# Making an exactness flag ahead of the last stores, and hinting the branch that depends on it

## The chip, the cores and the metric

The kernel runs on one core of a Trainium2 chip. Its metric is the device time of one execution in microseconds (us). That time is longer than the span that a profile shows, which goes from the first to the last instruction of the kernel.

Engines: PE is TensorE, DVE is VectorE, ACT is ScalarE, POOL is GpSimd, SP is SyncE. A small q (SPq) marks an instruction that the engine's sequencer handles alone.

Some words that recur: an *instruction packet* is a packet of a DMA queue that the profile lists as instruction (8 or 16 KB each in these traces); I read it as an engine's next instructions and call those of one packet a *block*. The *hole* behind a branch is the time from the start of the branch to the start of the engine's next instruction. The *issue* of a store is the time that SyncE spends on starting it, and the store has *landed* at the last landing that the profile records for it.

## The reference

```python
xn = layernorm(x)                          # 2048 x 512
s  = multi_query_attention(xn, wq, wk, wv) @ wo   # 32 heads of 16, softmax over 2048 keys
g  = silu((silu(xn @ w_gate) * (xn @ w_up)) @ w_down)
out = x + s * g
```

## The kernel before

The kernel computes the softmax without a row maximum. That is exact as long as the denominators stay in a range, so it checks them at the end: one flag, loaded into a register of every engine, and a branch. If the flag is set, an exact path with row maxima computes everything again. With these inputs it never is, and every engine jumps over the exact path. GpSimd has no instruction in that path, SyncE some 185, the others thousands (counted in e10_forced, the one run that executed it).

```python
    for i, o in enumerate(order):          # the body: instructions in a fixed order
        ...
        r = o.emit()
        chain(o.eng if o.eng != "DMA" else "SP", r)
    ...
    tadd("DVE", ...)                       # dlc = (denominators are in range)
    for k in range(2):
        tadd("PE", e_out_mm(LN + k, obk[k], [NQ - 1]))
    for k in range(2, 4):
        tadd("PE", e_out_mm(LN + k, obk[k], [NQ - 1]))
    tadd("DVE", e_out_mul(LN, obk[0], dsts[0]))
    fin_add(0, nc.gpsimd, "POOL")
    ...                                    # three more multiplies and adds
    fin_add(3, nc.vector, "DVE")
    for k in range(4):
        tadd("SP", e_out_st(LN + k))       # the last four stores
    tadd("DVE", nc.vector.tensor_reduce(out=fmin[:, 2:3], in_=dlc[:], ...))
    tadd("DVE", nc.vector.tensor_reduce(out=fmin[:, 3:4], in_=fmin[:, 0:3], ...))
    tadd("PE", nc.tensor.matmul(out=tq01[0:1, 0:1], lhsT=fmin[:, 3:4], rhs=ones_f[:], ...))
    tadd("DVE", nc.vector.tensor_single_scalar(out=flag_i[:], in_=tq01[0:1, 0:1], scalar=P - 0.5, op=ALU.is_lt))
    ...
    flag = nc.values_load(flag_i[0:1, 0:1], min_val=0, max_val=1)
    with tc.If(flag > 0):
        _exact_max_path(...)
```

`chain` and `tadd` fix the order of issue on one engine.

## Time and profile before

| | before |
|---|---|
| time, median of the first three runs | 783.76 us |
| span of the profiled run | 780.93 us |
| ScalarE, TensorE, VectorE busy | 97%, 96%, 94% |
| last VectorE add ends | 774.24 us |
| flag loaded by all engines from | 775.05 us |
| last store issued, landed | 774.27, 775.98 us |

The prediction shows the lines that carry this. The last 5.9 us have no computing at all: flag loads, the bounds check, a branch with a hole of 2.7 to 4.1 us on every engine but GpSimd (0.17 us), and the closing waits and barrier. One line of the store's source line (shortest, median and longest issue in ns):

```profile
L698 SPq DMA_DIRECT2D out_dram<-xn x4: 332/338/344, 772.2 to 774.3; - x4
```

### The profile page before, as it was taken

What the parts mean: (1) busy time and instruction counts of PE and PEld (TensorE: products, weight loads), DVE (VectorE), ACT (ScalarE), POOL (GpSimd) and SP (SyncE); (2) the same over time, 40 slices, a digit from 0 to 9 for tenths busy, and PEclk for the clock granted to TensorE, in tenths of its full rate; (3) what the DMA queues carried; (4) which work ended last, traced back from release to release, by engine and by line L of the source; (5) the groups of instructions that cost most, each with busy time, mean ns of one, the idle gap of its engine ahead of it and who ended that gap; (6) DMA issues with size and microseconds to landing.
All of it is one profiled execution on the core that took longest, in us unless ns stands there. A gap on an engine that the chain in (4) does not pass through costs nothing.

```text
span 780.9 us, 21436 instructions
## 1 busy us (share of the span) xinstructions
PE 749.8 (96%) x9095; PEld 230.2 (29%) x9095; DVE 735.7 (94%) x920; ACT 757.2 (97%) x866; POOL 53.5 (7%) x59
## 2 busy tenths in 40 slices
PE   8999999999999999999999999999999999999994
PEld 3323223322222333322232322222223333222221
DVE  7689999999999999999999999999999999999994
ACT  6999999999999999999999999999999999999992
POOL 2100000000012000000001110000000300000101
PEclk9999999999999999999999999999999999999997
DMA  9400000000001000000000100000000000000001
GB/s 329 139 8 9 16 2 24 2 8 17 6 27 49 24 2 8 17 2 24 3 10 29 42 23 2 24 1 9 17 2 24 29 22 2 3 23 2 23 2 32
DMA packets 21199, 20.20 MB, mean 26 GB/s; under 512 B 8744, under 2 KB 17192, under 8 KB 21096
## 3 DMA queue, kind: packets, MB, share of 16 engines
q1 hardware_dynamic: 19512, 18.20, 7.7%
q8 instruction: 73, 1.20, 0.6%
q10 hardware_dynamic: 1584, 0.56, 0.3%
q14 instruction: 30, 0.25, 0.1%
HBM read 14.19 MB, written 2.34 MB: 21 GB/s over the span
## 4 chain that ended last, share of the span: by engine, by line
PE 46%; ACT 38%; issue 8%; DVE 6%; SPq 0%; DMA 0%; ACTq 0%; POOL 0%; DVEq 0%; POOLq 0%
ACT Pb L937 33%; PE ring L877 17%; PE m_ps L488 15%; PE o_ps L747 13%; ACT th L657 3%; DVE Bf L991 2%; ACT g_sb L937 1%; DVE Bf L1010 1%; PE ring L433 1%; ACT th L674 1%; DVE x_sb L1010 0%; DVE x_sb L1005 0%; PE ring L488 0%; DVE hT L663 0%; DVE Bf L1005 0%
## 5 line engine op out<-in xcount | busy, mean ns | idle before, releaser
L937 ACT ACTIVATE Pb<-ring 128x1024 bf16<-128x1024 f32 x772 | 726.4, 1141 | 2.5 <-PE ring L877 2.3
L877 PE MATMUL ring<-QB,KT 32*128 32x512 bf16 x2048 | 306.1, 382 | 15.5 <-ACT Pb L937 8.9
L991 DVE TENSOR_SCALAR Bf<-ring 128x1024 uint16<-128x1024 f32 x172 | 209.6, 1218 | 5.4 <-PE ring L877 4.0
L877 PEld LDWEIGHTS <-KT 32*128 32x128 bf16 x2048 | 94.4, 91 | 314.1 <-issue 307.4
L747 PE MATMUL o_ps<-Pb,VA 128*32 128x512 bf16 x1544 | 146.9, 385 | 0.0
L1010 DVE TENSOR_TENSOR Bf<-Bf,Bf 128x2048 f16<-128x2048 f16 x74 | 90.3, 1220 | 0.1
L991 DVE TENSOR_SCALAR x_sb<-ring 128x1024 uint16<-128x1024 f32 x72 | 87.7, 1218 | 2.5 <-PE ring L877 2.1
L747 PE MATMUL o_ps<-xnT,zw 128*32 128x512 bf16 x1092 | 83.1, 381 | 0.0
L488 PE MATMUL m_ps<-xnT,wu_sb 128*32 128x512 bf16 x896 | 72.6, 384 | 0.8 <-DVE ab L659 0.6
L488 PE MATMUL m_ps<-wd_sb,hT 128*32 128x512 bf16 x896 | 71.5, 383 | 0.1
L488 PE MATMUL m_ps<-xnT,wg_sb 128*32 128x512 bf16 x896 | 70.4, 384 | 0.0
L747 PE MATMUL o_ps<-Bf,VD 128*32 128x512 f16 x688 | 67.1, 385 | 0.9 <-DVE Bf L1010 0.5
L732 POOL TENSOR_TENSOR oT<-oa,rb 128x512 bf16<-128x512 f32 x15 | 22.0, 1464 | 615.6 <-DMA rb<-dscr 409.2
L1017 DVE TENSOR_SCALAR Bf<-Bf 128x2048 uint16<-128x2048 uint16 x86 | 62.0, 721 | 0.6
L747 PEld LDWEIGHTS <-VA 128*32 128x32 bf16 x1560 | 38.0, 94 | 53.8 <-issue 51.5
L1005 DVE TENSOR_SCALAR Bf<-Bf 128x2048 uint16<-128x2048 uint16 x74 | 51.2, 700 | 0.0
L659 DVE SCALAR_TENSOR_TENSOR ab<-th,m_ps 128x512 f32<-128x512 f32 x56 | 38.1, 681 | 4.2 <-ACT th L657 3.9
L657 ACT ACTIVATE th<-m_ps 128x512 f32<-128x512 f32 x56 | 40.1, 716 | 0.0
L663 DVE TENSOR_TENSOR hT<-ab,m_ps 128x512 bf16<-128x512 f32 x56 | 38.2, 682 | 2.0 <-PE m_ps L488 1.6
L747 PEld LDWEIGHTS <-VD 128*32 128x32 f16 x976 | 26.5, 94 | 39.4 <-issue 35.8
L747 PEld LDWEIGHTS <-zw 128*32 128x32 bf16 x1092 | 25.8, 95 | 25.5 <-issue 12.9
L1010 DVE TENSOR_TENSOR x_sb<-x_sb 128x2048 f16<-128x2048 f16 x24 | 29.2, 1217 | 0.0
(121 smaller groups left out, 416.3 us busy)
## 6 DMA issues: line engine op xcount, KB each, us to landing
rb<-dscr SPq DMA_DIRECT2D x15, 256.0 KB
out_dram<-xn SPq DMA_DIRECT2D x16, 128.0 KB, 1.9
dn<-oa SPq DMA_DIRECT2D x120, 2.0 KB, 1.7
oa<-oa SPq DMA_DIRECT2D x60, 32.0 KB, 2.0
wg_sb<-in_B_w_gate_dram SPq DMA_DIRECT2D x1, 1792.0 KB, 11.5
wu_sb<-in_B_w_up_dram SPq DMA_DIRECT2D x1, 1792.0 KB
wd_sb<-in_B_w_down_dram SPq DMA_DIRECT2D x1, 1792.0 KB, 20.3
x_sb<-in_A_x_dram SPq DMA_DIRECT2D x3, 512.0 KB
```

The lines of the kernel that those rows point to most:

```text
L488: return [nc.tensor.matmul(out=dst[GRP * j:GRP * j + GRP, :], lhsT=w[:, GRP * j:GRP * j + GRP], rhs=rhs, start=start, stop=stop, tile_posi ...
L657: t_ = OP("ACT", 0.477, [a], lambda: nc.scalar.activation(out=th[i][:], in_=m_ps[:], func=ACT.Tanh, scale=0.5), (0,), name="tanh")
L659: s_ = OP("DVE", 0.6, [t_, ab_rel[i]], lambda: nc.vector.scalar_tensor_tensor(out=ab[i][:], in0=th[i][:], scalar=1.0, in1=m_ps[:], op0=ALU ...
L663: h = OP("DVE", 0.6, [b], lambda: nc.vector.tensor_tensor(out=hT[:, f, :], in0=ab[i][:], in1=m_ps[:], op=ALU.mult), (1,), name="hmul")
L732: return [pk, q], lambda eng: eng.tensor_tensor(out=oT[qs % 2][:, jj, :], in0=o0[:], in1=rbt[:], op=ALU.mult)
L747: r.append(nc.tensor.matmul(out=o_ps[GRP * g:GRP * g + GRP, :], lhsT=lhs, rhs=rhs, start=(n == 0), stop=(n == pv_total[(b, g)] - 1), tile_ ...
L877: return lambda: [nc.tensor.matmul(out=ring[sl][:, u * 512:(u + 1) * 512], lhsT=KT[half][GRP * g:GRP * g + GRP, t * P:(t + 1) * P], rhs=QB ...
L937: lambda: nc.scalar.activation(out=buf, in_=ring[i][:], func=ACT.Exp, scale=escale, bias=ebias),
L991: lambda: nc.vector.tensor_scalar(out=U[:, hs], in0=ring[si][:], scalar1=ubias, scalar2=UINF, op0=ALU.add, op1=ALU.min), (1.5, u), name="p ...
L1005: o1 = OP("DVE", 0.6, [pa, pa0] + wrel, lambda: nc.vector.tensor_scalar(out=Bf[wi], in0=U, scalar1=0x3FF, scalar2=0x3800, op0=ALU.bitwise_and,
L1010: return lambda: eng.tensor_tensor(out=Bf[wi][:, a:z].bitcast(FP16), in0=Bf[wi][:, a:z].bitcast(FP16), in1=U[:, a:z].bitcast(FP16), op=ALU ...
L1017: o2 = OP("DVE", 0.6, o3, lambda: nc.vector.tensor_scalar(out=U, in0=U, scalar1=0x7C00, scalar2=None, op0=ALU.bitwise_and), (2, u, 1), nam ...
```

## The change

Intent: make the flag before the last multiplies, load it before the stores, drop the check that it is 0 or 1, and give each engine a hint ahead of its branch, meant to have the branch's target fetched by then. The whole diff, moved lines shortened:

```diff
     tadd("DVE", nc.vector.tensor_tensor(out=dlc[:], in0=dlc[:], in1=dlf, op=ALU.is_equal))
+    tadd("DVE", nc.vector.tensor_reduce(out=fmin[:, 2:3], in_=dlc[:], ...))
+    tadd("DVE", nc.vector.tensor_reduce(out=fmin[:, 3:4], in_=fmin[:, 0:3], ...))
     ...
     for k in range(2):
         tadd("PE", e_out_mm(LN + k, obk[k], [NQ - 1]))
+    tadd("PE", nc.tensor.matmul(out=tq01[0:1, 0:1], lhsT=fmin[:, 3:4], rhs=ones_f[:], ...))
     for k in range(2, 4):
     ...
     tadd("DVE", e_out_mul(LN, obk[0], dsts[0]))
+    tadd("DVE", nc.vector.tensor_single_scalar(out=flag_i[:], ...))
+    for en, et in (("SP", "SP"), ("POOL", "Pool"), ("PE", "PE"), ("DVE", "DVE"), ("ACT", "Activation")):
+        with tc.issue_after(_last[en].ins):
+            tc.mark_branch_hint_location("exact", "LikelyTaken", [getattr(mybir.EngineType, et)])
+    loads, vals = nc.values_load_multi_w_load_instructions(flag_i[0:1, 0:1])
+    flag = vals[0]
+    tadd("SP", [l for l in loads if l.ins.engine == nc.sync.engine])
     fin_add(0, nc.gpsimd, "POOL")
     ...
     for k in range(4):
         tadd("SP", e_out_st(LN + k))
-    (the two reduces, the matmul and the compare)
-    flag = nc.values_load(flag_i[0:1, 0:1], min_val=0, max_val=1)
-    with tc.If(flag > 0):
+    with tc.If(flag > 0, label="exact"):
```

## The prediction

> **What bounds the kernel now.** I read the page first, for which part of the 780.9 us the change can touch at all. In the body ScalarE is busy 97%, TensorE 96% and VectorE 94%. The main row is 772 exponentials of 1141 ns on ScalarE. None of that is in the diff, and the order of the body is fixed by the kernel's own list, so I take everything up to the last block as unchanged. What is left is the end of the program. I cut it into stretches with the view of busy time by window:

> ```profile
> 766.00:770.00 4.00, 3.46 (x42) 1.26 (x33) 2.26 (x10) 1.02 (x3) 0.00 (x0) 1.00 0.01 4
> 770.00:772.00 2.00, 0.62 (x12) 0.12 (x8) 1.86 (x4) 0.00 (x0) 1.02 (x1) 1.00 0.00 0
> 772.00:775.00 3.00, 0.19 (x2) 0.09 (x2) 2.58 (x7) 0.00 (x0) 1.69 (x2) 0.50 0.40 131
> 775.00:778.00 3.00, 0.00 (x0) 0.00 (x0) 0.02 (x1) 0.00 (x0) 0.00 (x0) 0.50 0.20 58
> 778.00:780.90 2.90, 0.00 (x0) 0.00 (x0) 0.00 (x0) 0.00 (x0) 0.00 (x0) 0.50 0.05 14
> ```

> The columns are the stretch and its length, then busy us and count for TensorE, its weight load, VectorE, ScalarE and GpSimd, then clock, DMA share and GB/s. From 770 to 775 VectorE sets the pace (1.86 of 2, 2.58 of 3). After 775 there are 5.9 us in which no engine computes. So I looked at the instructions that do not count as busy, by the line of the flag load and of the branch:

> ```profile
> L1367 SPq TENSOR_LOAD <-flag_i x1: 482/482/482, 775.1 to 775.1; - x1
> ...
> L1367 SPq FUSED_REGOPS  x1: 192/192/192, 775.6 to 775.6; - x1
> L1367 SPq SEQ_ASSERT  x1: 37/37/37, 775.8 to 775.8; - x1
> ```

> ```profile
> L1368 SPq EVENT_SEMAPHORE  x8: 17/17/17, 779.0 to 779.5; - x8
> L1368 ACTq COMPARE_BRANCH  x1: 50/50/50, 775.6 to 775.6; - x1
> ...
> L1368 PEldq COMPARE_BRANCH  x1: 4038/4038/4038, 775.7 to 775.7; - x1
> L1368 DVEq COMPARE_BRANCH  x1: 72/72/72, 775.7 to 775.7; - x1
> L1368 SPq COMPARE_BRANCH  x1: 50/50/50, 776.2 to 776.2; - x1
> L1368 ACTq EVENT_SEMAPHORE  x1: 17/17/17, 778.4 to 778.4; - x1
> L1368 DVEq EVENT_SEMAPHORE  x1: 21/21/21, 778.8 to 778.8; - x1
> ```

> The three numbers are the shortest, median and longest duration in ns. Every engine loads the flag at 775.05, when VectorE has just made it, in 0.47 to 0.54 us. Then all branch over the exact path. SyncE branches only at 776.24, after the two bounds-check instructions, and the next instruction that it executes starts at 778.99: 2.7 us of nothing. ScalarE has the same hole from 775.64 to 778.40 and VectorE from 775.75 to 778.81; TensorE shows it inside the branch itself, 4.04 us. The trace's instruction-fetch packets (8 KB for SyncE, ScalarE and VectorE, 16 KB for TensorE) run from 776.54 to 778.27, so the hole is the fetch of the branch's target. SyncE's waits say that nothing else holds it:

> ```profile
> SPq L1368 <- SPq L1368: 2.7, 1, 2.7
> SPq L1396 <- PEq L1396: 0.7, 2, 0.5
> ```

> The last store was issued at 774.27 and had landed by 775.98 (1.71 us), before any of this. From SyncE's second semaphore wait after the branch (779.085) to the last instruction (ends 780.93) there are 1.85 us: seven more waits at 0.07, eight double waits at 0.06 each, drains, two rounds of the closing barrier.

> So the chain that ends the program is: last VectorE add, two reduces, a tiny matmul, the compare, the flag load, the bounds check, the branch, the fetch, SyncE's closing waits.

> [...]

> **The change, part by part.** (1) *Flag ahead of the stores.* The two reduces (172 and 156 ns) move to where VectorE idles for 0.63 us before its first multiply (770.14), waiting for TensorE: they cost nothing. The fp32 matmul (two passes, 0.19 us together) goes between the output matmuls at about 770.0; it pushes outputs 2 and 3 by perhaps 0.1 us, and they are finished 0.9 us before VectorE needs them. The compare (146 ns, about 0.2 us from start to start, as the small neighbours at 769.12 and 769.32 are spaced) sits between the first and second multiply of a VectorE that is back to back from 770.14 to 774.24. So the last add ends 0.2 us later, at 774.44. What leaves the path behind the add is 774.24 to 775.05: 0.8 us of reduces, matmul and compare. (2) *Load ahead of the stores.* SyncE's load ends near 771.6, before the first store's data (772.14): free. The 0.48 us leave the end. (3) *No bounds check*: 775.60 to 776.24, about 0.65 us, leaves; but with the load moved it would have stood beside VectorE's work anyway. (4) *Hints.* TensorE and ScalarE now branch near 771.7 and would be through their own fetches by 775.9 and 774.6 even unhinted. VectorE would need till about 776.9. Only SyncE, which branches after the fourth store (774.47 + 0.34 + 0.05 = 774.86), would have its 2.7 us at the end: resume at 777.55.

> New end without a working hint: 777.55 plus the 1.95 us from SyncE's resuming to the end (778.985 to 780.93) = 779.5, a gain of 1.4 us. With the hint SyncE goes on at once and meets the last store instead: issued 774.47, landed 774.47 + 1.71 = 776.18, plus 1.85 us of closing = 778.03, a gain of 2.9 us. That is the central step: the fetch is replaced by the landing of the last store, and half of the hint's 2.7 us is lost to it.

> **Rivals.** *A, VectorE's own flag load gets in the way.* Only SyncE's load is chained. VectorE loads the flag too; if that stands right behind the compare, its sequencer waits for the compare and then 0.54 us, and everything behind moves by some 0.6 us: gain 2.3. For it: it is traced there. Against: in the opening of the trace a VectorE operation that waits for GpSimd is placed behind later-written memsets, so what is ready sooner goes first, and the second multiply is ready. Behind that multiply, the load would mostly hide beside 0.68 us of execution. *B, GpSimd's load stands ahead of its first add*: the add starts at 771.6 in place of 770.98, both GpSimd adds move 0.6 us, and stores 2 and 3 are issued in order behind them: gain about 2.4. *C, the hint does nothing[...]* before SyncE branches: gain 1.4. Only some ten SyncE instructions stand between hint and branch, which speaks against it. *D, the hints hurt*: [...] gain about 0, or a small loss. *E, the prediction that the eye makes*, all 5.9 us gone: impossible, since 1.71 + 1.85 us after the last store remain.

> **Range and chances.** Weights: all as worked out 0.5 (783.76 - 2.9 = 780.9), A or B 0.3 (781.4), C 0.12 (782.4), D 0.08 (783.8). The median is about 781.1. The three runs of before spread by 0.5 us, so the range is 780.4 to 782.4. A 2% change would be 15.7 us; the whole tail is 5.9 us, so neither side of 2% is within reach unless the body's order changed, which the fixed list speaks against.

> **What would show it right or wrong.** Right: the body to 770 us unchanged; SyncE's first semaphore wait comes under 0.2 us after its branch; its wait for the last store ends 1.7 us after that store's issue; last add at 774.4; the span near 778.0. Wrong in step 1: the second multiply starts later than 771.0, with a flag load on VectorE before it. B: GpSimd's load before its first add. C: SyncE still has a hole of 2.7 us behind the branch, and instruction packets lie after it. D: a new hole between hint and branch. Wrong altogether: a body that ended earlier or later by over 1 us.

The gain is 2.9 us, so the time 783.76 - 2.9 = 780.9 us with weight 0.5, and beside it stand the rivals' 781.4 (0.3), 782.4 (0.12) and 783.8 (0.08), for a median near 781.1. That a working hint lets SyncE go on at once was the change's claim; no trace taken before the prediction has a hint in it. The weights, the loss in D and the use made of the ten SyncE instructions in C were my estimates.

## More of the kernel before

All runs but one were fast, with a granted TensorE clock of 0.99 or more; the exception, e10_forced, is no timing.

A *far* branch is one that jumps over the exact path.

## The result, and the profile after

The median is 781.57 us (six runs, 780.87 to 782.02) against 783.49 us (six runs). The ratio is 0.9974, 95% interval 0.9961 to 0.9987, the class "same" at 2% (no difference of 2% or more is shown; that holds for every timed experiment below too). A ratio is the mean time of one kernel's fast runs over that of the other's of the same rounds, so it is not quite the ratio of the medians. The time fell inside the predicted range. The reason given for it did not hold.

First the part that went as predicted. The view is VectorE's timeline of the changed kernel (start, length, what):

```profile
769.97 0.69 DVE L690 SCALAR_TENSOR_TENSOR ab<-ring,g_sb 128x512 f32<-128x512 f32 x1 [0.22 <-PE ring L488]
770.57 0.14 DVE L1354 TENSOR_SCALAR flag_i<-ring 1x1 int32<-1x1 f32 x1
770.64 0.67 DVE L690 SCALAR_TENSOR_TENSOR ab<-ring,g_sb 128x512 f32<-128x512 f32 x1
```

The compare sits between the first two multiplies, and the second starts only 0.67 us after the first (0.61 us before the change). From the copy of the last attention block to the end of the last add it is 7.50 us, against 7.48 before: the flag is free. The flag loads of the changed kernel:

```profile
L1358 SPq TENSOR_LOAD <-flag_i x1: 474/474/474, 770.7 to 770.7; - x1
...
L1358 POOLq TENSOR_LOAD <-flag_i x1: 501/501/501, 771.9 to 771.9; - x1
L1358 DVEq TENSOR_LOAD <-flag_i x1: 543/543/543, 773.2 to 773.2; - x1
```

GpSimd's load came after its first add and VectorE's after the last add was issued, so rivals A and B did not happen. Now hints and branches of the changed kernel:

```profile
L1400 SPq BRANCH_PREFETCH_HINT  x1: 56/56/56, 733.9 to 733.9; - x1
...
L1400 ACTq BRANCH_PREFETCH_HINT  x1: 45/45/45, 769.4 to 769.4; - x1
L1400 PEldq BRANCH_PREFETCH_HINT  x1: 50/50/50, 769.9 to 769.9; - x1
L1400 DVEq BRANCH_PREFETCH_HINT  x1: 56/56/56, 770.1 to 770.1; - x1
```

```profile
L1372 SPq EVENT_SEMAPHORE  x8: 17/17/17, 777.9 to 778.8; - x8
L1372 ACTq COMPARE_BRANCH  x1: 68/68/68, 771.3 to 771.3; - x1
L1372 PEldq COMPARE_BRANCH  x1: 3705/3705/3705, 771.3 to 771.3; - x1
...
L1372 ACTq EVENT_SEMAPHORE  x1: 17/17/17, 773.9 to 773.9; - x1
...
L1372 SPq COMPARE_BRANCH  x1: 70/70/70, 775.3 to 775.3; - x1
```

The hints were executed, and every hole is still there: 2.6 us on ScalarE, 3.8 on TensorE, 2.5 on SyncE (775.35 to 777.85). The DMA view of the window from 766.9 to 771.9 us, which holds three of the hints and the first two branches, shows that nothing was fetched:

```profile
DMA packets 0, 0.00 MB, mean 0 GB/s; under 512 B 0, under 2 KB 0, under 8 KB 0
```

The first instruction packets come at 772.23 (ScalarE) and 772.37 (TensorE), about 1 us after the branches, as in the kernel before. SyncE's hint had executed at 733.9, 41 us ahead of its branch, and the trace has no 8 KB packet between it and 772.23. This is rival C.

And something new. The stores of the changed kernel, to be read against the same line of before:

```profile
L698 SPq DMA_DIRECT2D out_dram<-xn x4: 348/579/1392, 772.0 to 774.5; - x4
```

The second store's issue takes 1.39 us and the fourth's 0.80, each 0.33 to 0.34 before. The last store lands at 778.37, 3.87 us after its issue at 774.50 (before: 1.71). In this profile SyncE is past its hole at 777.85 and then waits for that landing until 778.39; from there it is 1.84 us to the end at 780.23.

The profiled execution was the slowest of the six. Its span is only 0.7 us shorter than that of the profiled execution of before, its time 2.2 us shorter (782.02 against 784.17), and this difference is the last surprise. Time minus span, from each run's list:

| | mean time | mean span | time minus span: mean, lowest, highest |
|---|---|---|---|
| before (9 runs, chip of the control) | 783.50 | 780.87 | 2.63, 1.88, 3.17 |
| changed (5 runs, same chip: the control below) | 781.55 | 779.72 | 1.83, 1.80, 1.85 |

Of the gain of 1.95 us, 1.15 lie in the kernel's span and 0.80 in the closing work after its last instruction. The second part depends on the chip: before's time minus span is 2.98 on average on the chip of e1, 2.63 here.

### The profile page after: what moved, and what is told of

Its sections match the earlier page's. It is cut to its first block, busy times and chain, and to the rows that moved or that the text cites. A ratio compares the mean times of both kernels' runs of the same rounds, so it can differ in the third digit from the quotient of the medians.

```text
span 780.2 us, 21438 instructions
## 1 busy us (share of the span) xinstructions
PE 748.7 (96%) x9095; PEld 229.7 (29%) x9095; DVE 733.9 (94%) x920; ACT 757.1 (97%) x866; POOL 53.0 (7%) x59
## 4 chain that ended last, share of the span: by engine, by line
PE 47%; ACT 37%; issue 8%; DVE 6%; POOL 0%; SPq 0%; DMA 0%; ACTq 0%; DVEq 0%; POOLq 0%
ACT Pb L937 33%; PE ring L877 17%; PE m_ps L488 15%; PE o_ps L747 13%; ACT th L657 3%; DVE Bf L991 1%; ACT g_sb L937 1%; ACT th L674 1%; DVE Bf L1010 1%; DVE x_sb L1010 0%; PE ring L488 0%; DVE Bf L1005 0%; DVE Bf L1017 0%; DVE x_sb L991 0%; DVE x_sb L1005 0%
```

## The experiments

"Gain" is the mean time of the kernel before minus that of the experiment, on the same chip (e1, e3, e4 and e5 share one, e11 has its own, the others share a third). Across chips I compare gains; since before's closing work differs by 0.35 us between the first and the third chip, the gain in the span is the steadier of the two. All results were correct.

| run | what | median us | gain | of it in the span |
|---|---|---|---|---|
| c0_after | changed kernel again | 781.63 | 1.95 | 1.15 |
| e1_no_hints | changed, no hints | 781.35 | 2.25 | 1.07 |
| e2_check_kept | changed, bounds check back | 781.76 | 1.95 | 1.15 |
| e3_tiny_body | changed, exact path one memset | 779.22 | 4.32 | 3.13 |
| e4_sp_near | changed, nothing for SyncE to jump over | 781.80 | 2.45 | 1.29 |
| e5_hints_early | changed, hints ahead of the last block fetch | 780.47 | 3.13 | 1.97 |
| e6_early_held | e5, branches held until the last add | 779.17 | 4.16 | 3.37 |
| e7_early_held_near | e6 and e4 | 779.18 | 4.33 | 3.59 |
| e8_before_early | before, with early hints only | 782.97 | 0.59 | -0.29 |
| e9_after_crossing | changed, hints early but after the last block fetch | 781.37 | 2.14 | 1.28 |
| e11_before_early_nocheck | e8 without bounds check | 779.37 | 3.96 | 3.04 |

**c0_after**, no edit:

> The changed kernel itself, as the measure on this chip for the three others: 781.0 to 781.9, and again no instruction packet within 1.5 us after the hints, holes of 2.5 to 3.7 us behind the branches.

It gave 781.63 us (780.60 to 782.34), with no packet behind the hints again and holes of 2.7 to 3.5 us. Issues of 1.16 us and a last landing 2.86 us after its issue show that the stores are slowed in another execution too, by another amount.

**e1_no_hints**: are the late hints of any use?

```diff
-    for en, et in (("SP", "SP"), ...):
-        with tc.issue_after(_last[en].ins):
-            tc.mark_branch_hint_location("exact", "LikelyTaken", ...)
```

> The changed kernel without its five branch hints. Theory (the hints fetched nothing; the trace of the changed kernel has no instruction packet between the hints at 769.4 to 770.2 us and 0.9 us after the first branch): the same time within 0.5 us, 781.2 to 781.9, and the same holes behind the branches, 2.5 us on ScalarE and SyncE, 3.1 us on VectorE, 3.7 us inside TensorE's branch. Rival (the hints shorten a part of the fetch that the packets do not show): 0.5 to 1.5 us slower than the changed kernel, and the holes back at 2.8, 2.7, 3.1 and 4.1 us.

The time is the same as the changed kernel's (781.35 us, 780.70 to 782.05). Holes: ScalarE 2.6, VectorE 3.1, SyncE 2.7, TensorE 4.1. TensorE's is 0.4 to 0.6 us longer than in the runs with late hints, but the kernel before also had 4.1, and packet and branch stand 1.6 us apart here and 1.0 in the kernel before, so I read no effect out of it. The late hints are worth nothing that these runs can see.

**e5_hints_early**: do hints work at all? At every engine's chosen place in the body loop:

```diff
+    early = {"SP": (430.0, "SP"), "DVE": (688.0, "DVE"), "ACT": (712.0, "Activation"), "PE": (758.0, "PE"), "POOL": (712.0, "Pool")}
+    sc_t = order[-1].start / 766.0
     for i, o in enumerate(order):
+        for en, (tt, et) in list(early.items()):
+            if o.start > tt * sc_t:
+                with tc.issue_after(_last[en].ins):
+                    tc.mark_branch_hint_location("exact", "LikelyTaken", [getattr(mybir.EngineType, et)])
+                early.pop(en)
     ...
-    (the late hints)
```

The places come from the trace. It does not name a packet's engine; I tell it from the size and the spacing. In the kernel before, 8 KB packets start when ScalarE has started 65, 193, 321, 449, 576 and so on to 1601 of its recorded instructions, 125 to 130 apart; VectorE's are some 128 apart too (122 to 134), SyncE's 129 (79 and 208). The 16 KB ones, which I take for TensorE's, come 9 to 13 us apart in the body. The last such fetch before the branch was near 456 us for SyncE, 702 for VectorE, 730 for ScalarE and 765 for TensorE.

> The changed kernel with each hint moved earlier, ahead of the last time that its engine goes over to a new block of instructions (SyncE some 430 us, VectorE 688, ScalarE 712, TensorE 758 of the span). Theory A (a hint only takes effect when the engine's prefetcher next fetches a block, so the late hints came too late to be served): no hole behind the branches (under 0.3 us), no instruction packets after 771 us until the engines have branched, last store landed 1.7 us after its issue, span near 777.8, time 779.0 to 779.6. Theory B (the hints do nothing here at all): the same as without hints, 781.2 to 781.9, holes of 2.5 to 3.7 us.

The branches of this run:

```profile
L1377 ACTq COMPARE_BRANCH  x1: 68/68/68, 770.9 to 770.9; - x1
L1377 PEldq COMPARE_BRANCH  x1: 425/425/425, 771.0 to 771.0; - x1
L1377 ACTq EVENT_SEMAPHORE  x1: 17/17/17, 771.4 to 771.4; - x1
...
L1377 DVEq COMPARE_BRANCH  x1: 84/84/84, 773.4 to 773.4; - x1
L1377 DVEq EVENT_SEMAPHORE  x1: 21/21/21, 774.0 to 774.0; - x1
```

The hints work. ScalarE's hole falls from 2.6 to 0.49 us, TensorE's from 3.8 to 0.48, VectorE's from 3.2 to 0.62. SyncE now waits only for store landings. The holes are 0.5 us and not under 0.3, so a taken hinted branch is not free. The time is 780.47 us, later than expected, because the collision did not go: packets at 771.99 and 772.11 lie beside the stores, the second store's issue takes 1.46 us and the last one lands 2.52 us after its issue. I take these packets for the blocks that follow the targets, since they start a short and steady time after the engines go on: 0.6 us on ScalarE and VectorE (771.38 to 771.99, 774.01 to 774.59), 0.7 us on TensorE in this run (771.44 to 772.11) and 0.7 to 1.1 us in the others. The kernel before has them too, at 779.00, 779.40 and 779.55, about 0.6 us after ScalarE, VectorE and SyncE go on (778.40, 778.81, 778.99).

**e4_sp_near**: what is SyncE's own jump worth?

```diff
 # in _exact_max_path, three times
-                nc.sync.dma_start(...)
+                nc.scalar.dma_start(...)
```

> The changed kernel with the DMAs of the exact path issued by ScalarE in place of SyncE, so that SyncE has nothing to jump over and its branch target lies next to the branch. Theory (SyncE's fetch is the last hole on the path; behind it stands only the landing of the last store): SyncE's hole goes from 2.5 to under 0.3 us as GpSimd's, the end is then the last store's landing plus 1.85 us, time 779.3 to 780.5, by as much as the store is still slowed by other engines' instruction packets. Rival (VectorE's or TensorE's fetch, ending at 776.9 and 775.1, or the landing alone sets the end): within 0.5 us of the changed kernel.

The five times are 779.94, 780.52, 781.80, 781.85 and 782.08 us: not one population. The profile caught the fastest, in which SyncE waits only for stores (until 776.29) and the end follows 1.86 us later, as the theory has it. What the three slow executions waited for, no profile shows. Alone this run is inconclusive.

**e3_tiny_body**: no far jump; is there still a fetch?

```diff
     with tc.If(flag > 0, label="exact"):
-        _exact_max_path(...)
+        nc.vector.memset(eps_t[:], EPS)
```

> The changed kernel with the exact path cut down to one memset (right on these inputs, since the path is not taken; it has no fallback). Flag, loads, branches and stores stay; no branch goes far, so nothing has to be fetched. Theory (the changed kernel's 1.39 and 0.80 us store issues and the 3.9 us from the last store's issue to its landing come from instruction fetches[...]): all four issues back at 0.33 to 0.36 us, landing 1.7 us after issue, span 777.7 to 778.2, time 779.0 to 779.7. Rival (the issues are slowed by GpSimd's work or by the flag loads beside them): issues still at 0.8 us and over, end 0.5 to 1 us later, 779.8 to 780.5.

The issues are 0.33 to 0.35 us and the landing 1.72 us, at 779.22 us. One 8 KB packet, at 773.30, is left. With so small a block the instruction scheduler put the branch ahead of three of the stores, so the order is not the changed kernel's and this is not a clean bound. It shows rival A on the way: VectorE's flag load and branch stood in front of its remaining work, and from the attention copy to the last add it was 8.26 us in place of 7.50: 0.8 us, where the prediction gave the load alone 0.6.

**e6_early_held**: take the packets away from the stores.

```diff
+    # the three lines of the flag load moved down to just ahead of the stores
+    _sync = mybir.DependencyInfo(mybir.DependencyClass.Sync, mybir.DependencyReason.DATA)
+    for l in loads:
+        if l.ins.engine in (nc.tensor.engine, nc.scalar.engine, nc.vector.engine):
+            tc.add_manual_dep(l.ins, _last["DVE"].ins.name, _sync, reason="hold")
     for k in range(4):
         tadd("SP", e_out_st(LN + k))
```

> The kernel with the early hints, and with the flag loads of TensorE, ScalarE and VectorE made to wait for VectorE's last add, so that their branches and the block fetches that follow them come after the stores are issued. Theory (the changed kernel and the early-hint kernel lose 0.5 to 1 us because instruction packets, TensorE's 16 KB one above all, hold up SyncE's store issues and landings): all four store issues at 0.33 to 0.39 us (1.46 us for the second one with early hints alone), last store landed 1.7 to 2.0 us after its issue, 0.5 to 0.8 us faster than early hints alone: 779.6 to 780.1. Rival (the slow issues come from SyncE's own state, or the held engines now end last): the second issue is still over 1 us, or the end comes from TensorE's branch; time 780.4 or more.

The DMA view of this run from 766.9 to 775.2 us (packets; then the queue's), and its stores:

```profile
DMA packets 576, 0.52 MB, mean 63 GB/s; under 512 B 64, under 2 KB 576, under 8 KB 576
...
q1 hardware_dynamic: 576, 0.52, 19.2%
```

```profile
L698 SPq DMA_DIRECT2D out_dram<-xn x4: 332/338/348, 771.7 to 773.8; - x4
DMA to landing us min/median/max: 1.7/1.7/1.7
```

No instruction packet is left there, all four issues are short, the last store lands 1.72 us after its issue, and the end follows 1.86 us after that: the end that the prediction had drawn for the changed kernel. The gain is 4.16 us, 1.0 us more than with early hints alone, and 1.4 us more in the span. The edit moved two things, the flag loads and the branches with the packets that follow them. The loads are not what slows a store: in this run three of them (773.81 to 774.50) lie beside the fourth store, whose issue takes 0.33 us. So the instruction packets are what slowed the stores. The traces say more: in seven runs (the changed kernel, c0, e1, e2, e4, e5, e9) SyncE's longest issue ended 0.30 to 0.38 us after TensorE's 16 KB packet did. Four of them, and this run:

| run | TensorE's packet ends | SyncE's longest issue ends |
|---|---|---|
| changed kernel | 773.55 | 773.92 |
| e1_no_hints | 773.70 | 774.08 |
| e5_hints_early | 773.26 | 773.61 |
| e9_after_crossing | 773.25 | 773.61 |
| e6_early_held | none there | no long issue |

The 8 KB packets may have their part: the changed kernel's fourth issue (774.50 to 775.31) lies beside two of them (774.48 to 775.48), and no run separates the two sizes. How a packet holds an issue up is not shown.

**e7_early_held_near**: both edits.

> The same as the held kernel, and the exact path's DMAs issued by ScalarE, so that SyncE neither jumps far nor fetches a target. Theory (with a hint that works SyncE's branch is already hidden behind the last store's landing): within 0.3 us of the held kernel. Rival (SyncE's remaining 0.5 us behind the branch, or its own block fetch colliding with the last store, still counts): 0.3 to 0.6 us faster than the held kernel.

The median is 779.18 us against 779.17: SyncE's hinted jump is hidden behind the last landing.

**e2_check_kept**: is the bounds check worth anything here?

```diff
-    ...values_load_multi_w_load_instructions(flag_i[0:1, 0:1])
+    ...values_load_multi_w_load_instructions(flag_i[0:1, 0:1], min_val=0, max_val=1)
```

> The changed kernel with the bounds check put back on the early flag load (two more SyncE instructions, 0.65 us in the kernel before). Theory (SyncE waits for the first store's data anyway after its early load): the check ends before 772.2 us, the first store is issued at most 0.2 us later, the last one at the same time; the time within 0.4 us of the changed kernel on the same chip. Rival (the check is where the gain came from): 0.6 us slower or more.

The check ends at 771.26, 0.4 us before the first store can be issued, and the gain is that of the control; that it is so to the hundredth is chance, as the five executions spread by over 1.6 us. Removing the check gave the changed kernel nothing that these runs can see. One thing stays open: SyncE's hole is 1.93 us here, against 2.5 in the changed kernel, and its packet starts 0.26 us after the branch, against 0.96.

**e9_after_crossing**: is it lead time or the block fetch that a hint needs?

```diff
-    early = {"SP": (430.0, "SP"), "DVE": (688.0, "DVE"), "ACT": (712.0, ...), "PE": (758.0, "PE"), ...}
+    early = {"SP": (600.0, "SP"), "DVE": (715.0, "DVE"), "ACT": (742.0, ...), ...}   # PE: after the transposes, 767.0
```

> The early-hint kernel, but each hint moved to just after its engine's last block fetch, still well ahead of the branch: ScalarE near 742 us (last block fetch near 730), VectorE near 715 (near 702), SyncE near 600 (near 456), TensorE near 767.5 (near 765). Theory (a hint is only served at the next block fetch, and none comes before the branch): no packet follows a hint, holes of 2.5 to 3.7 us on ScalarE, VectorE and TensorE, the time of the changed kernel, 781.0 to 781.9. Rival (a hint starts a fetch of its own and only needs a lead of some us, which the late hints lacked): a packet within 2 us of each hint, holes of about 0.5 us, the time of the early hints, 780.4 to 780.9.

Its branches:

```profile
L1379 ACTq COMPARE_BRANCH  x1: 68/68/68, 770.9 to 770.9; - x1
L1379 PEldq COMPARE_BRANCH  x1: 499/499/499, 771.0 to 771.0; - x1
L1379 PEldq EVENT_SEMAPHORE  x1: 51/51/51, 771.5 to 771.5; - x1
...
L1379 ACTq EVENT_SEMAPHORE  x1: 17/17/17, 773.8 to 773.8; - x1
```

**e8_before_early**: the early hints alone, flag and check at the end.

```diff
 # the kernel before, with the `early` lines of e5 and label="exact"
```

> The kernel before with nothing but the early hints: flag, bounds check and loads stay at the end. Theory (early hints take the fetch out of the branch): the holes go to 0.49 us on ScalarE, 0.48 on TensorE, 0.62 on VectorE; SyncE branches near 776.2 as before and goes on about 0.5 us later in place of 2.7, then 1.95 us to the end: 2.1 to 2.3 us faster than before, 781.2 to 781.6, about as much as the flag's move alone gives. Rival (the hints only help since the branches of the other engines lie early): less than 1 us faster.

ScalarE, TensorE and VectorE have the short holes. SyncE has not; SyncE's waits in this run:

```profile
SPq L1375 <- SPq L1375: 3.3, 1, 3.3
```

The span is no shorter than before's (781.13 on average against 780.84). Still the time is 0.6 us better, all of it after the span: time minus span is 1.74 to 1.85 in its six runs, and 1.88 to 3.30 in before's. In this run TensorE goes on at 775.8 and its next block's packet comes at 776.46; in before it goes on at 779.76 and the packet runs from 780.68 to 781.79, past the last instruction at 780.93. It fits that what follows the kernel waited for TensorE's instructions in before, and no longer does in any variant in which TensorE is past its branch early. It is not shown: e8 moved ScalarE and VectorE on as well, no run moved TensorE alone, and the closing work itself has no instructions in the profile.

**e11_before_early_nocheck**: why did SyncE miss?

```diff
-    flag = nc.values_load(flag_i[0:1, 0:1], min_val=0, max_val=1)
+    flag = nc.values_load(flag_i[0:1, 0:1])
```

> The kernel before with the early hints and without the bounds check; flag and loads stay at the end. With the check SyncE missed its hinted block (hole 3.35 us): its branch was its instruction 336 of the trace, and its block fetches come after instructions 78 and 206, so the next after 334. Theory (the two check instructions pushed the branch over the next block boundary[...]): SyncE's branch is instruction 334 and its hole about 0.5 us; it branches near 775.2, goes on near 775.7, and the end is 1.95 us later: span 777.6 to 777.9, time 779.2 to 779.9. Rival (SyncE's hint works only where the flag is loaded early): hole 2.5 us or more, gain over the kernel with early hints and check at most 0.7 us, 782.2 to 782.7.

SyncE's waits:

```profile
SPq L1375 <- SPq L1375: 0.5, 1, 0.5
```

As expected: hole 0.51 us, span 777.58. Two SyncE instructions less make 3.4 us (gain 3.96 against 0.59), some 0.65 of it their own time and the rest the hinted block. The branch is SyncE's recorded instruction 334 here and 336 in e8, with block fetches every 128 (after 78 and 206): the boundary lies between. That it is the boundary, and not the check instructions as such, that costs SyncE its hint is not shown: it would need other instructions in their place, which I did not run.

**e10_forced**, one look: the fallback of e6 with the threshold raised so that the flag is always set.

```diff
-    ... scalar=P - 0.5, op=ALU.is_lt
+    ... scalar=P + 0.5, op=ALU.is_lt
```

> The held kernel with the threshold of the compare raised by one, so that the flag is always set and the exact path always runs, hinted as not taken. It is no timing: it shows whether the fallback of that kernel still gives the reference's result[...]. Expected: correct; a time longer by over 1 ms, as the whole attention is done again.

It is correct, at 3947 us: the wrong hint did not spoil the result. Most of this time is the exact path itself; what the wrong hint costs, this run does not separate.

The best versions are e6 and e7 (0.9948 and 0.9945 of before, where the changed kernel is 0.9976 on that chip). e11 comes to 0.9949 on another chip and is the simplest: the kernel before, hints at the right places, no bounds check, and the flag left where it was.

## Why the prediction was right or wrong

- **What bounds the tail: right.** The chain over SyncE's branch and the dependence of the closing waits on it are what the runs moved. The fixed 1.85 us after SyncE's last-store wait measured 1.84 to 1.86 us wherever the landing set the end.
- **The flag is free: right.** Predicted 0.2 us for the compare; between the two multiplies it was 0.06, and the last add came 7.50 us after the attention copy against 7.48.
- **The load ahead of the stores and the bounds check: right.** Both stood beside VectorE's work (e2: same gain with the check). But that the check costs nothing depends on the flag's place: with the flag at the end it decided whether SyncE's hint helped (hole of 3.35 us in e8 with the check, 0.51 us in e11 without).
- **The central step failed**: "the fetch is replaced by the landing of the last store". With the change as written no fetch is replaced; the late hints fetch nothing. I had given this (rival C) 0.12. My argument against it, that only some ten SyncE instructions stand between hint and branch, was the wrong way round: so few instructions meant that the hint stood behind SyncE's last block fetch (near 456 us), and there it did nothing, although it was 41 us ahead of the branch (e9: 180 us ahead, and nothing). The step itself is sound where a hint works: e6 ends landing + 1.86 us.
- **Rival C's size**: 1.4 us of span predicted, 1.15 measured on average. The rest went to instruction packets beside the stores, a new cost that no rival named: an issue up to 1.1 us longer and a landing up to 2.2 us slower. In the profile SyncE branched at 775.35 and not at 774.86, and after its hole it waited 0.5 us more for the landing. The prediction took the landing at 1.71 us from a trace in which the fetches came after the stores.
- **What made up for it**: 0.8 us of the measured gain (on the control's chip) lie outside the span. I had set a gain in span equal to a gain in time. With C alone that would have given 782.4; the measured median was 781.57.
- **A and B did not happen** in the changed kernel; the order argument held. A's size was seen in e3 (0.8 us for a predicted 0.6).

That the range held was luck, then: the central step was missing, and a smaller gain in the span, a cost that nobody had named and a gain outside the span came to a time within it.

## What to carry to other kernels

In this kernel a far branch cost its engine a hole of 1.9 to 4.1 us, and a prefetch hint left 0.5 to 0.6 us of it where it stood ahead of that engine's last block fetch before the branch (the exception is SyncE in e8, with a hole of 3.35 us; on TensorE one hint behind that fetch, 4.0 us ahead of the branch, worked as well, and one 1.4 us ahead did not). Where a hint is tried, check it by the hole behind the branch and by the instruction packets, and check again after adding or removing instructions: two fewer on SyncE were worth 3.4 us here (e8 against e11). Choose where branches fall so that the fetches do not run beside the last stores: that was worth 1.0 us here (e5 against e6). Look at time minus span as well as at the span: an edit can change what follows the kernel, as 0.6 us of e8 do, all of it after the span.
